# One weight copy, one normalisation pass and four folding transfers in the feed-forward half of an attention + SoLU kernel

## The chip, the cores and the metric

The kernel runs on one core of one Trainium2 chip. The metric is the time on the device in microseconds (us) of one execution, inputs and outputs in the chip's main memory. A core has five engines that run their own instruction queues side by side: PE (matrix multiply; its weight loads are shown as PEld), DVE, ACT and POOL (element-wise work) and SP, which here only issues transfers (DMAs). The engines wait for one another through semaphores. PE writes its results to PSUM, which has eight banks; everything else lies in SBUF, 128 partitions wide.

## The reference, cut to what matters

Everything is float32 except `w_in` and `w_out`, which come as 64-bit floats and are taken apart on the chip.

```python
def _attn_ref(q, k, v, tau):            # q, k, v: (8, 8, 576, 64)
    scores = scale * np.matmul(q, k.transpose(0, 1, 3, 2))
    thresh = np.max(scores, axis=-1, keepdims=True) - tau
    scores = np.where(scores >= thresh, scores, -1000000000.0)
    scores = scores - np.max(scores, axis=-1, keepdims=True)
    attn = np.exp(scores)
    attn = attn / (np.sum(attn, axis=-1, keepdims=True) + 1e-09)
    return np.matmul(attn, v)

def _moe_ref(x, w_in, w_out, g_ln):     # x: (4608, 512), w_in: (512, 1024), w_out: (1024, 512)
    h = x @ w_in
    e = np.exp(h - np.max(h, axis=-1, keepdims=True))
    solu = h * (e / (np.sum(e, axis=-1, keepdims=True) + 1e-09))
    mu = np.mean(solu, axis=-1, keepdims=True)
    var = np.mean((solu - mu) ** 2, axis=-1, keepdims=True)
    ln = (solu - mu) / np.sqrt(var + 1e-06) * g_ln
    return ln @ w_out
```

The attention output of the 8 heads, laid side by side, is `x`: 8 x 576 = 4608 tokens of 512 features.

## The kernel before, in words

**Rounds.** The program is written out by a Python loop over rounds (`rnd`, lines 898 to 1059). Each of the first 144 rounds (`NS`) takes one slot of attention: the scores of 128 query rows of two heads (`scores`, L480), their row maximum on DVE (`maxes`, L502), a threshold and an exponential on ACT (`ramp`, L517; `exps`, L526), a scaling on POOL one round later (`normalise`, L533 to L536), and a 32 x 32 block transpose on DVE (`blocks`, L548). After every second slot SP issues three or four transfers (L557, L559, L564) that fold the transposed weights `T` into `wT`, so that keys lie on the partitions. About three rounds later `attend_steps` (L590) multiplies with `v`, and ACT copies the result into the token tile `xh` or `xe` (L622). Each batch has 16 slots for its first 512 rows and two more for its last 64.

**The feed-forward half** works on 36 units of 128 tokens. A unit `t` takes four rounds of PE: `ff_h` twice (L655, or L645 near the end), then `ff_o` twice (L760, part 0 and part 1 in two consecutive rounds). Between its h and its o lie, each in a round of its own: `ff_max` and `ff_exp` (L670, L679), `ff_mul` and `ff_sum` (L685, L690, L691), `ff_stats` (L700 to L711), `ff_norm`, `ff_norm2` and `ff_swap`, and `ff_turn`. While one unit is in its h rounds, the unit before it is normalised and turned, and then has its o rounds. So the rounds go h, h, o, o in the middle of the kernel, with scores at the head of each round, and the h rounds also hold the attention products. The last scores are in round 144; after that the rounds hold only feed-forward steps, and the two parts of an o follow each other on PE with nothing between them.

**The path from u to o.** After `ff_mul` the tile `u` holds 128 tokens on the partitions and 1024 features. `ff_norm` (ACT, L721) writes the normalised values to `V`, `ff_norm2` (DVE, L726) writes the same values back over `u`. `ff_swap` issues four transfers on SP (L737); each moves 32 partitions x 512 features from `u` into `V`, so that after a block transpose on DVE (`ff_turn`, L747) the partitions 0 to 63 hold 64 features of the tokens 0 to 63, and the partitions 64 to 127 those of the tokens 64 to 127. `u`, `V` and (but for the end) `uT` have one buffer each.

**ff_o before.** Sixteen steps `m`, eight in each part. In each step, row half `r` (64 partitions) holds one half of the tokens, so it needs all of `w_out` by itself: `w2` holds `w_out` twice, the second time with its 64-partition halves exchanged (`weight_d`, L332: two transfers for each of eight pieces). Row half `r` always writes its own bank:

```python
out=d["o"][ROWS[z], 512 * (r ^ other) : 512 * (r ^ other) + 256],
lhsT=d["uT"][ROWS[r], m].rearrange("p y x -> p (y x)"),
rhs=w2[ROWS[r], m ^ r, 256 * z : 256 * z + 256],
```

**ff_h before, for comparison.** Its row halves hold different input features of the same tokens, so both add into the same results. In part 0 row half 0 writes bank 0 and row half 1 bank 1, in part 1 they exchange. `fence` (L109) is a POOL memset of a 128 x 1 tile that waits for the last four matmuls of part 0; the first matmul of part 1 waits for it. Units whose h falls at the end (`split` false, L645) use whole 128-row matmuls and need no fence.

**Start.** In rounds 0 to 15 the sixteen pieces of the 64-bit weights are loaded (512 KB each, `weight_load`, L275), taken apart (L286 to L325, on DVE, ACT and POOL), and for `w_out` multiplied with the gain `g_ln` in `gs`, whose rows are loaded once (L878) and turned on PE (`gains`). SP issues nearly all transfers in program order; each reuses one of eight semaphores, and waits until the transfer that had it before has landed.

Of the kernel before, what the change touches and what calls it, by code (L numbers as in the profile page):

```python
# [8 lines left out]
F32 = mybir.dt.float32  # L9
# [3 lines left out]
AF = mybir.ActivationFunctionType  # L13
# [7 lines left out]
def kernel(  # L21
# [47 lines left out]
    ident = const.tile([P, P], F32, name="ident")  # L69
    swapped = const.tile([P, 64], F32, name="swapped")  # L70
    w1 = const.tile([P, NP, DFF], F32, name="w1")
    w2 = const.tile([P, 2 * NC, DM], F32, name="w2")
    w1_parts = w1.rearrange("p c (a g x) -> p c g a x", g=2, x=32)
    mhalf = const.tile([P, 1], F32, name="mhalf")
    mone = const.tile([P, 2], F32, name="mone")
    mark = const.tile([P, 1], F32, name="mark")
# [181 lines left out]
    def piece(x):  # L258
        if x < 2 * NP:
            c, hf = divmod(x, 2)  # L260
            cols = slice(512 * hf, 512 * hf + 512)
            return w_in[P * c : P * c + P, cols], w1[:, c, cols], W_UNIT
        c = x - 2 * NP
        return w_out[P * c : P * c + P], w2[:, 2 * c], gs[:, c : c + 1]

    NW = 2 * NP + NC
    raws = {}
# [54 lines left out]
    def weight_gain(x):  # L322
        if wide and x >= 2 * NP:
            e = raws[x]["em"][0].bitcast(F32)
            nc.scalar.activation(out=e, in_=e, func=AF.Copy, scale=piece(x)[2])  # L325


    def weight_d(x):
        c = x - 2 * NP
        if c >= 0:  # L330
            for r in range(2):
                nc.sync.dma_start(out=w2[ROWS[r], 2 * c + 1], in_=w2[ROWS[1 - r], 2 * c])  # L332

    SPARE = 7
# [263 lines left out]
    def attended(key):  # L601
        b, kind, hp = key
        tag, y = units.pop(key)["y"]
        y = y.rearrange("p (u n) -> p u n", u=2)[:, :, 0:P]
        if kind == 2 or b < 2:
            y = y.rearrange("p u (r y) -> p u r y", r=2)
        else:
            y = y.rearrange("p u (g r x) -> p u g r x", g=2, r=2)
        if kind == 2:
            if b % 2 == 0:  # L610
                xe[b // 2] = work.tile([P, NP, P], F32, tag="xe", bufs=1, name="xe")
            to = xe[b // 2][:, :, 64 * (b % 2) : 64 * (b % 2) + 64].rearrange(
                "p (u r) y -> p u r y", u=2
            )
        else:
            if hp == 0:
                xh[b, kind] = work.tile(
                    [P, NP, 256], F32, tag=f"xh{(2 * b + kind) % 4}", bufs=1, name="xh"
                )
            how = "p (r u y) -> p u r y" if b < 2 else "p (u g x r) -> p u g r x"  # L620
            to = xh[b, kind][:, hp].rearrange(how, u=2, r=2, **({} if b < 2 else {"g": 2}))
        nc.scalar.copy(out=to, in_=y)  # L622
        pairs_free.append(tag)
# [92 lines left out]
    def ff_norm(t):  # L716
        d = ffn[t]
        rs, nb = d["norm"]
        d["V"] = V = work.tile([P, 2, DFF // 2], F32, tag="V", bufs=1, name="V")
        u = d["u"].rearrange("p (g n) -> p g n", g=2)  # L720
        nc.scalar.activation(out=V, in_=u, func=AF.Identity, bias=nb, scale=rs)  # L721

    def ff_norm2(t):
        d = ffn[t]
        rs, nb = d["norm"]
        nc.vector.tensor_scalar(  # L726
            out=d["u"], in0=d["u"], scalar1=rs, scalar2=nb, op0=ALU.mult, op1=ALU.add
        )

    def ff_swap(t):
        d = ffn[t]
        for g in range(2):
            for r in range(2):
                to, of = 64 * r + 32 * g, 64 * r + 32 * (1 - g)
                nc.sync.dma_start(  # L737
                    out=d["V"][to : to + 32, 1 - g],
                    in_=d["u"][of : of + 32, DFF // 2 * g : DFF // 2 * g + DFF // 2],
                )  # L740

    def ff_turn(t, rnd):
        d = ffn[t]
        turns.append(t)
        tag = "xh0" if rnd > NS and len(turns) % 2 else "uT"
        d["uT"] = uT = work.tile([P, 2 * NC, 2, 32], F32, tag=tag, bufs=1, name="uT")
        nc.vector.transpose(  # L747
            out=uT, in_=d["V"].rearrange("p y (m x) -> p m y x", x=32)
        )
        d["turned"] = rnd + 1  # L750

    def ff_o(t, part):
        d = ffn[t]
        other = len(t) == 3 and t[0] > 1 and t[2]
        if part == 0:
            d["otag"], d["o"] = take("o_ps")
        for m in range(NC * part, NC * part + NC):
            for r in range(2):
                for z in range(2):
                    nc.tensor.matmul(  # L760
                        out=d["o"][ROWS[z], 512 * (r ^ other) : 512 * (r ^ other) + 256],
                        lhsT=d["uT"][ROWS[r], m].rearrange("p y x -> p (y x)"),
                        rhs=w2[ROWS[r], m ^ r, 256 * z : 256 * z + 256],
                        start=m == 0, stop=m == 2 * NC - 1,
                    )

    def ff_out(t, last):
        d = ffn[t]
# [8 lines left out]

    def ff_store(t, last):
        d = ffn.pop(t)
        if len(t) == 1:  # L780
            of = slice(2 * t[0], 2 * t[0] + 2)
            if t[0] == 0:
                rows = out.rearrange("(b s) m -> s b m", s=S)[SM:S, of]
            else:
                rows = out.rearrange("(b k t) m -> k t b m", b=B, t=NK)[:, NK - 1, of]
        elif t[0] > 1:
            b, kind, m = t
            rows = out[b * S : b * S + S, :].rearrange("(k t) m -> k t m", t=NK)
            rows = rows[:, 4 * kind + 2 * m : 4 * kind + 2 * m + 2]
        else:  # L790
            b, kind, m = t
            rows = out[b * S : b * S + SM, :].rearrange("(p t) m -> t p m", t=4)
            rows = rows[2 * kind + m].rearrange("(r k) m -> k r m", r=2)
        for z in range(2):
            (nc.scalar if last and z else nc.sync).dma_start(
                out=rows[:, :, 256 * z : 256 * z + 256],
                in_=d["ob"][ROWS[z]].rearrange("p (r n) -> p r n", r=2),
            )


    NS = len(slots)
# [66 lines left out]
    with tc.manual_schedule():  # L868
# [29 lines left out]
        while True:  # L898
# [89 lines left out]
            if step == ("h", 0):  # L988
                ff_h(cur, 0, rnd + 1 < NS, beside)
                quarter = 1  # L990
            elif step == ("h", 1):
                ff_h(cur, 1, None, beside)
                quarter = 2
                by = rnd + 2 * (rnd == 14)
                late.setdefault(by, []).append(lambda t=cur: (ff_max(t), ff_exp(t)))
                late.setdefault(by + 1, []).append(lambda t=cur: (ff_mul(t), ff_sum(t)))
                middle.setdefault(by + 2, []).append(lambda t=cur: ff_stats(t))
                if rnd + 6 < NS:
                    norms[by + 3] = cur
                else:  # L1000
                    late.setdefault(rnd + 2, []).append(lambda t=cur: ff_norm(t))
                middle.setdefault(by + 3, []).append(lambda t=cur: (ff_norm2(t), ff_swap(t)))

                at = by + 4 if more or not ready or len(ready[0][1][0]) == 1 else rnd + 6
                if cur == (0, 1, 1):
                    middle.setdefault(rnd + 6, []).append(lambda t=cur, at=rnd + 6: ff_turn(t, at))
                else:
                    late.setdefault(at, []).append(lambda t=cur, at=at: ff_turn(t, at))
                if not more:
                    between.append(cur)  # L1010
                    cur = None
                    quarter = 0
            elif step == ("o", 0):
                if prev is not None:
                    ff_o(prev, 0)
                quarter = 3
            elif step == ("o", 1):
                if prev is not None:
                    ff_o(prev, 1)
                    last = not (more or ready or cur or between)  # L1020
                    begin.setdefault(rnd + 1, []).append(lambda t=prev, last=last: ff_out(t, last))
                    late.setdefault(rnd + 1, []).append(lambda t=prev, last=last: ff_store(t, last))
                prev, cur = cur, None
                quarter = 0
# [68 lines left out]
```

## Time and profile before

| | |
|---|---|
| median of 3 runs | 861.14 us |
| lowest, highest | 861.04, 863.58 us |
| the profiled execution, first to last instruction (its span) | 867.2 us |
| PE busy | 822.9 us, 95% of the span |
| DVE, ACT, POOL busy | 681.7, 573.6, 500.2 us |
| transfers | 168.54 MB, mean 194 GB/s |
| L760, matmuls of o | 4608, busy 271.6 us |
| L726, second normalisation on DVE | 36, mean 982 ns |
| L721, normalisation on ACT | 36, mean 1241 ns |
| L109, the fences of h on POOL | 32, mean 98 ns |

The profile gives no time of the profiled execution but its span; that lies 6.1 us above the median of the runs shown. "Busy" counts the time in which an engine has at least one instruction under way. Matmuls overlap one another, so a PE that is busy is not always at its full rate; the number of matmuls in a stretch says more. A line such as `L760` is line 760 of the kernel printed above. In a timeline, a bracket at the end of a line gives the engine's idle time before that instruction and what ended it.

### The profile page before, as it was taken

The page shows a single profiled execution, that of the slowest core. Times are in us where ns is not written, and L with a number is a line of the kernel's source. Part 1 is how long each engine was busy: PE and PEld are TensorE (multiplying, and loading weights), DVE is VectorE, ACT ScalarE, POOL GpSimd, SP SyncE. Part 2 cuts the span into 40 slices and gives each one's busy share as a digit, 9 for nine tenths or more (in the row PEclk, how much of TensorE's full clock was granted, in tenths as well). Part 3 has the DMA queues.
Part 4 walks back from the last instruction along what each step waited for, and adds up shares of the span by engine and source line. Part 5 has one row for each costly group of instructions (what it writes and reads, how often), then busy time and mean ns, then how long its engine had stood idle before and what let it go on. Part 6 is the DMA issues. An engine that isn't in the chain of part 4 may idle for free.

```text
span 867.2 us, 36122 instructions
## 1 busy us (share of the span) xinstructions
PE 822.9 (95%) x15361; PEld 605.8 (70%) x15361; DVE 681.7 (79%) x1248; ACT 573.6 (66%) x1153; POOL 500.2 (58%) x938
## 2 busy tenths in 40 slices
PE   5668799989999999999999999999999999999997
PEld 3446466667677776899777766777777777777655
DVE  4988878878788888888888887888788887787361
ACT  5877876667677767777666766777677776776121
POOL 2886656556756666565656665565666655555120
PEclk9769999999999999999999999999999999999999
DMA  8999887998888878898888787888788787655312
GB/s 256 252 251 227 191 210 181 210 236 210 215 206 226 208 183 214 208 221 203 196 207 225 207 187 185 217 220 207 183 230 229 197 192 180 163 136 139 69 38 62
DMA packets 83712, 168.54 MB, mean 194 GB/s; under 512 B 15448, under 2 KB 45152, under 8 KB 83552
## 3 DMA queue, kind: packets, MB, share of 16 engines
q1 hardware_dynamic: 82416, 164.25, 76.3%
q8 instruction: 120, 1.97, 1.0%
q10 hardware_dynamic: 1136, 2.00, 0.7%
q14 instruction: 40, 0.33, 0.1%
HBM read 46.14 MB, written 9.44 MB: 64 GB/s over the span
## 4 chain that ended last, share of the span: by engine, by line
PE 79%; DMA 8%; DVE 4%; ACT 4%; SPq 2%; issue 2%; POOL 1%; ACTq 0%; DVEq 0%
PE o_ps L760 26%; PE h_ps L655 20%; PE pv L590 14%; PE s_ps L480 14%; DMA wT<-T 6%; PE h_ps L645 3%; ACT w L517 1%; DVE w L502 1%; ACT w L526 1%; DVE T L548 1%; DMA q<-in_q_dram 1%; DMA qT<-flip 1%; SPq L564 1%; DMA k<-in_k_dram 1%; SPq L559 0%
## 5 line engine op out<-in xcount | busy, mean ns | idle before, releaser
L760 PE MATMUL o_ps<-w,uT 64*64 64x256 f32 x4608 | 271.6, 378 | 1.2 <-ACT xe L622 0.6
L502 DVE CUSTOM_DVE_ANT_0 w<-s_ps,tau_t 128x576 f32<-128x576 f32 x280 | 200.0, 751 | 90.0 <-PE s_ps L480 61.6
L517 ACT ACTIVATE w<-s_ps,nth 128x576 f32<-128x576 f32 x280 | 196.9, 739 | 107.0 <-DVE nth L502 89.6
L760 PEld LDWEIGHTS o_ps<-w,uT 64*64 64x64 f32 x4608 | 212.7, 134 | 66.1 <-ACT xh L622 12.1
L536 POOL TENSOR_SCALAR w<-w,sm 128x576 f32<-128x576 f32 x288 | 222.1, 783 | 14.3
L548 DVE STREAM_TRANSPOSE T<-w 128x576 f32<-128x576 f32 x288 | 207.6, 755 | 20.6 <-POOL w L536 19.1
L655 PE MATMUL h_ps<-w,xh 64*64 64x512 f32 x1856 | 221.0, 589 | 0.1
L526 ACT ACTIVATE w<-w,ntau 128x576 f32<-128x576 f32 x288 | 219.7, 767 | 0.0
L590 PEld LDWEIGHTS pv<-wT,v 64*64 64x64 f32 x5760 | 175.2, 138 | 45.4 <-issue 24.5
L480 PE MATMUL s_ps<-kT,qT 64*64 64x64 f32 (+1 forms) x2048 | 177.1, 422 | 13.3 <-ACT w L517 10.9
L590 PE MATMUL pv<-wT,v 64*64 64x128 f32 (+1 forms) x5760 | 178.0, 266 | 10.9 <-DMA wT<-T 7.8
L655 PEld LDWEIGHTS h_ps<-w,xh 64*64 64x64 f32 x1856 | 118.0, 133 | 78.8 <-issue 45.7
L533 POOL TENSOR_SCALAR sm<-sm 128x2 f32<-128x2 f32 x144 | 37.0, 257 | 201.8 <-ACT w L526 198.5
L534 POOL TENSOR_TENSOR sm<-sm,mone 128x2 f32<-128x2 f32 x144 | 108.7, 755 | 12.0
L480 PEld LDWEIGHTS s_ps<-kT,qT 64*64 64x64 f32 x2048 | 73.0, 139 | 21.7 <-ACT w L517 15.7
L622 ACT COPY xh<-pv 128x256 f32<-128x256 f32 x64 | 25.1, 393 | 82.4 <-PE pv L590 82.4
L721 ACT ACTIVATE V<-u,nb,rs 128x1024 f32<-128x1024 f32 x36 | 44.7, 1241 | 39.3 <-POOL nb L711 32.4
L747 DVE STREAM_TRANSPOSE uT<-V 128x1024 f32<-128x1024 f32 x36 | 44.2, 1227 | 18.1 <-DMA V<-u 17.7
L526 ACT ACTIVATION_READ_ACCUMULATOR w<-w,ntau 128x1 f32 x288 | 55.6, 193 | 0.0
L685 DVE TENSOR_TENSOR u<-h_ps,u 128x1024 f32<-128x1024 f32 x36 | 42.8, 1190 | 9.8 <-ACT u L679 9.8
L726 DVE TENSOR_SCALAR u<-u,rs,nb 128x1024 f32<-128x1024 f32 x36 | 35.3, 982 | 17.6 <-ACT V L721 17.6
L670 DVE TENSOR_REDUCE hm<-h_ps 128x1 f32<-128x1024 f32 x36 | 42.9, 1192 | 4.8 <-PE h_ps L645 2.7
(90 smaller groups left out, 568.1 us busy)
## 6 DMA issues: line engine op xcount, KB each, us to landing
wT<-T SPq DMA_DIRECT2D x160, 288.0 KB, 6.7
wT<-T SPq DMA_DIRECT2D x64, 576.0 KB, 5.4
V<-u SPq DMA_DIRECT2D x144, 64.0 KB, 3.3
out_dram<-ob SPq DMA_DIRECT2D x71, 128.0 KB, 2.5
q<-in_q_dram SPq DMA_DIRECT2D x24, 288.0 KB, 5.7
qT<-flip SPq DMA_DIRECT2D x48, 144.0 KB, 4.2
k<-in_k_dram SPq DMA_DIRECT2D x24, 288.0 KB, 6.1
kT<-flip SPq DMA_DIRECT2D x48, 144.0 KB, 3.9
```

Source lines behind the costliest of these rows:

```text
L480: nc.tensor.matmul(out=ps[h][ROWS[y], ks], lhsT=lhsT, rhs=d["kT"][ROWS[h], ks], start=True, stop=True,)
L502: nc.vector.tensor_tensor_reduce(out=w, in0=ps[:, 0:S], in1=(zero if loose else tau_t).to_broadcast([P, S]), scale=1.0, scalar=BIG, op0=AL ...
L517: nc.scalar.activation(out=d["w"][x], in_=d["w"][x] if d["loose"] else d["ps"][x][:, 0:S], func=AF.Prelu, bias=d["nth"][x], scale=-1.0, al ...
L526: nc.scalar.activation(out=w, in_=w, func=AF.Exp, bias=ntau, scale=1.0, accum_out=sm[:, x : x + 1])
L534: nc.gpsimd.tensor_tensor(out=sm, in0=sm, in1=mone, op=ALU.pow)
L536: nc.gpsimd.tensor_scalar(out=w, in0=w, scalar1=sm[:, x : x + 1], scalar2=1.0, op0=ALU.mult, op1=ALU.mult)
L548: nc.vector.transpose(out=T[:, :, r, h, :], in_=w)
L590: nc.tensor.matmul(out=to, lhsT=d["v"][ROWS[u], (h0 + h - u) % 4 if b > 1 else h0 + h, m ^ 4 * u if m < 8 and b < 2 else m,], rhs=rhs, sta ...
L655: mm = nc.tensor.matmul(out=h[ROWS[y], f], lhsT=x[ROWS[r], c, ROWS[y]], rhs=w1_parts[ROWS[r], c, part ^ r], start=part == 0 and c == 0, st ...
L721: nc.scalar.activation(out=V, in_=u, func=AF.Identity, bias=nb, scale=rs)
L747: nc.vector.transpose(out=uT, in_=d["V"].rearrange("p y (m x) -> p m y x", x=32))
L760: nc.tensor.matmul(out=d["o"][ROWS[z], 512 * (r ^ other) : 512 * (r ^ other) + 256], lhsT=d["uT"][ROWS[r], m].rearrange("p y x -> p (y x)" ...
```

## The change

`w2` holds `w_out` once, with the rows ordered so that the partition `32 b + i` of piece `m` is row `256 b + 32 m + i`; `weight_d` and its sixteen transfers are gone. The gain rows are loaded by four small transfers in that order. `ff_norm` normalises `u` in place on ACT, and `ff_norm2` is gone. `ff_fold` takes the place of `ff_swap`: each of its four transfers moves a quarter of the features of all 128 tokens (128 KB) into 32 partitions of `V`. The same block transpose then leaves 128 different features on the partitions in each of eight steps, for all 128 tokens. `ff_o` adds the two row halves into the same results, as `ff_h` does: eight steps in part 0, a fence, and the same eight steps in part 1 with the banks exchanged. The token order inside a unit changes with the fold, so the copies into `xh` and `xe` use another order, and the stores write whole 2 KB rows. `w1_parts` becomes two plain halves.

```diff
-    w2 = const.tile([P, 2 * NC, DM], F32, name="w2")
-    w1_parts = w1.rearrange("p c (a g x) -> p c g a x", g=2, x=32)
+    w2 = const.tile([P, NC, DM], F32, name="w2")
+    w1_parts = w1.rearrange("p c (g n) -> p c g n", g=2)
...
-        return w_out[P * c : P * c + P], w2[:, 2 * c], gs[:, c : c + 1]
+        rows = w_out.rearrange("(b m i) n -> m b i n", b=4, i=32)
+        return rows[c], w2[:, c], gs[:, c : c + 1]
...
-    def weight_d(x):
-        c = x - 2 * NP
-        if c >= 0:
-            for r in range(2):
-                nc.sync.dma_start(out=w2[ROWS[r], 2 * c + 1], in_=w2[ROWS[1 - r], 2 * c])
...
-            to = xe[b // 2][:, :, 64 * (b % 2) : 64 * (b % 2) + 64].rearrange(
-                "p (u r) y -> p u r y", u=2
-            )
+            y = y.rearrange("p u r (k e) -> p u r k e", e=2)
+            to = xe[b // 2].rearrange("p (u r) (k w e) -> p w u r k e", u=2, w=2, e=2)[:, b % 2]
...
-            how = "p (r u y) -> p u r y" if b < 2 else "p (u g x r) -> p u g r x"
+            how = "p (r u y) -> p u r y" if b < 2 else "p (g x u r) -> p u g r x"
...
     def ff_norm(t):
         d = ffn[t]
         rs, nb = d["norm"]
-        d["V"] = V = work.tile([P, 2, DFF // 2], F32, tag="V", bufs=1, name="V")
-        u = d["u"].rearrange("p (g n) -> p g n", g=2)
-        nc.scalar.activation(out=V, in_=u, func=AF.Identity, bias=nb, scale=rs)
-
-    def ff_norm2(t):
+        nc.scalar.activation(out=d["u"], in_=d["u"], func=AF.Identity, bias=nb, scale=rs)
+
+    def ff_fold(t):
         d = ffn[t]
-        rs, nb = d["norm"]
-        nc.vector.tensor_scalar(
-            out=d["u"], in0=d["u"], scalar1=rs, scalar2=nb, op0=ALU.mult, op1=ALU.add
-        )
-    def ff_swap(t):
...
+        d["V"] = V = work.tile([P, 4, DFF // 4], F32, tag="V", bufs=1, name="V")
+        for b in range(4):
+            nc.sync.dma_start(
+                out=V[32 * b : 32 * b + 32], in_=d["u"][:, 256 * b : 256 * b + 256]
+            )
...
-        d["uT"] = uT = work.tile([P, 2 * NC, 2, 32], F32, tag=tag, bufs=1, name="uT")
+        d["uT"] = uT = work.tile([P, NC, 4, 32], F32, tag=tag, bufs=1, name="uT")
...
     def ff_o(t, part):
         d = ffn[t]
-        other = len(t) == 3 and t[0] > 1 and t[2]
         if part == 0:
             d["otag"], d["o"] = take("o_ps")
-        for m in range(NC * part, NC * part + NC):
+        uT = d["uT"].rearrange("p m a x -> p m (a x)")
+        last = []
+        for m in range(NC):
             for r in range(2):
+                f = part ^ r
                 for z in range(2):
-                    nc.tensor.matmul(
-                        out=d["o"][ROWS[z], 512 * (r ^ other) : 512 * (r ^ other) + 256],
-                        lhsT=d["uT"][ROWS[r], m].rearrange("p y x -> p (y x)"),
-                        rhs=w2[ROWS[r], m ^ r, 256 * z : 256 * z + 256],
-                        start=m == 0, stop=m == 2 * NC - 1,
+                    mm = nc.tensor.matmul(
+                        out=d["o"][ROWS[z], 512 * f : 512 * f + 256],
+                        lhsT=uT[ROWS[r], m, ROWS[z]],
+                        rhs=w2[ROWS[r], m, 256 * f : 256 * f + 256],
+                        start=part == 0 and m == 0, stop=part == 1 and m == NC - 1,
                     )
+                    if part and not last:
+                        sync(mm, d["ofence"])
+                    last.append(mm)
+        if part == 0:
+            d["ofence"] = fence(last[-4:])
...
-        for z in range(2):
-            (nc.scalar if last and z else nc.sync).dma_start(
-                out=rows[:, :, 256 * z : 256 * z + 256],
-                in_=d["ob"][ROWS[z]].rearrange("p (r n) -> p r n", r=2),
-            )
+        for z, rows in enumerate(halves):
+            (nc.scalar if last and z else nc.sync).dma_start(out=rows, in_=d["ob"][ROWS[z]])
...
-        nc.sync.dma_start(out=g_rows, in_=g_ln.rearrange("(c p) -> c p", p=P))
+        for b in range(4):
+            nc.sync.dma_start(
+                out=g_rows[:, 32 * b : 32 * b + 32],
+                in_=g_ln.rearrange("(b m i) -> b m i", b=4, i=32)[b],
+            )
...
-                middle.setdefault(by + 3, []).append(lambda t=cur: (ff_norm2(t), ff_swap(t)))
+                middle.setdefault(by + 3, []).append(lambda t=cur: ff_fold(t))
...
-                weight_d(pieces[rnd - 1])
```

More of the change, by code (lines that the diff above doesn't have):

```diff
@@ L718, in ff_norm @@
         rs, nb = d["norm"]
-        d["V"] = V = work.tile([P, 2, DFF // 2], F32, tag="V", bufs=1, name="V")
-        u = d["u"].rearrange("p (g n) -> p g n", g=2)
-        nc.scalar.activation(out=V, in_=u, func=AF.Identity, bias=nb, scale=rs)
-    def ff_norm2(t):
+        nc.scalar.activation(out=d["u"], in_=d["u"], func=AF.Identity, bias=nb, scale=rs)
+    def ff_fold(t):
         d = ffn[t]
-        rs, nb = d["norm"]
-        nc.vector.tensor_scalar(
-            out=d["u"], in0=d["u"], scalar1=rs, scalar2=nb, op0=ALU.mult, op1=ALU.add
-        )
-    def ff_swap(t):
[L733 to L739, printed above, removed]
-                )
+        d["V"] = V = work.tile([P, 4, DFF // 4], F32, tag="V", bufs=1, name="V")
[3 more added lines that the diff above has]
+            )
     def ff_turn(t, rnd):
@@ L745, in ff_turn @@
         tag = "xh0" if rnd > NS and len(turns) % 2 else "uT"
-        d["uT"] = uT = work.tile([P, 2 * NC, 2, 32], F32, tag=tag, bufs=1, name="uT")
+        d["uT"] = uT = work.tile([P, NC, 4, 32], F32, tag=tag, bufs=1, name="uT")
         nc.vector.transpose(
-            out=uT, in_=d["V"].rearrange("p y (m x) -> p m y x", x=32)
+            out=uT, in_=d["V"].rearrange("p a (m x) -> p m a x", x=32)
         )
@@ L779, in ff_store @@
         d = ffn.pop(t)
+        halves = []
         if len(t) == 1:
[L781 to L785, printed above, removed]
+            for b in (2 * t[0], 2 * t[0] + 1):
+                if t[0] == 0:
+                    rows = out[b * S + SM : b * S + S, :].rearrange("(k e) m -> e k m", e=2)
+                else:
+                    rows = out[b * S : b * S + S, :].rearrange("(k e t) m -> t e k m", t=NK, e=2)
+                    rows = rows[NK - 1]
+                halves.append(rows)
         elif t[0] > 1:
             b, kind, m = t
-            rows = out[b * S : b * S + S, :].rearrange("(k t) m -> k t m", t=NK)
-            rows = rows[:, 4 * kind + 2 * m : 4 * kind + 2 * m + 2]
+            rows = out[b * S : b * S + S, :].rearrange("(k e t) m -> t e k m", t=NK, e=2)
+            halves = [rows[4 * kind + x] for x in ((0, 3), (1, 2))[m]]
         else:
             b, kind, m = t
-            rows = out[b * S : b * S + SM, :].rearrange("(p t) m -> t p m", t=4)
-            rows = rows[2 * kind + m].rearrange("(r k) m -> k r m", r=2)
-        for z in range(2):
-            (nc.scalar if last and z else nc.sync).dma_start(
-                out=rows[:, :, 256 * z : 256 * z + 256],
-                in_=d["ob"][ROWS[z]].rearrange("p (r n) -> p r n", r=2),
-            )
+            rows = out[b * S : b * S + SM, :].rearrange("(k a t) m -> t a k m", t=4, a=4)
+            rows = rows[2 * kind + m]
+            halves = [rows[0:2], rows[2:4]]
+        for z, rows in enumerate(halves):
+            (nc.scalar if last and z else nc.sync).dma_start(out=rows, in_=d["ob"][ROWS[z]])
     NS = len(slots)
```

## The prediction

> **What bounds the kernel now.** I read the engines' busy shares and the 40 slices first, then busy time by stage, to see where PE still has idle time that a change could win.
>
> ```profile
> PE 822.9 (95%) x15361; PEld 605.8 (70%) x15361; DVE 681.7 (79%) x1248; ACT 573.6 (66%) x1153; POOL 500.2 (58%) x938
> ...
> PE   5668799989999999999999999999999999999997
> ```
>
> ```profile
> 0.00:60.00 60.00, 36.01 (x615) 23.02 (x619) 47.13 (x103) 44.35 (x97) 38.88 (x59) 0.81 0.93 254
> ...
> 90.00:110.00 20.00, 14.88 (x332) 9.47 (x328) 17.37 (x34) 17.84 (x45) 13.76 (x21) 0.88 0.80 190
> ...
> 260.00:520.00 260.00, 259.44 (x4934) 202.66 (x4932) 217.39 (x393) 181.67 (x360) 158.62 (x310) 1.00 0.83 207
> 520.00:780.00 260.00, 258.43 (x4942) 193.91 (x4938) 213.67 (x388) 180.55 (x357) 156.53 (x302) 1.00 0.77 195
> ...
> 812.00:855.00 43.00, 43.00 (x660) 26.94 (x654) 19.20 (x23) 10.27 (x14) 7.11 (x21) 1.00 0.20 45
> ```
>
> The columns of the second view are the stretch, its length, busy us (and instructions) of PE, PEld, DVE, ACT and POOL, the granted clock, the DMA share and GB/s. From 260 to 780 us PE idles 2.1 us of 520 at full clock: taking 35 us off DVE cannot help there. PE idles 24 us in the first 60, 5.1 between 90 and 110, and not at all from 812 to 855. So the middle and the tail can only lose, and only the start can win.
>
> Is PE at its rate where it is busy? The chain that ended last closes with the o steps of the last four units, without a gap:
>
> ```profile
> 834.57 27.83 PE o_ps L760 x512
> ```
>
> That is 27.83 / 512 = 54 ns from one matmul to the next, while one lasts 376 ns (median of L760). Seven are under way together, so making PE run empty once costs about 376 - 54 = 0.32 us before any waiting.
>
> A steady pair of o rounds, in order of time (start, length, engine, line, what):
>
> ```profile
> 499.76 3.20 PE L760 MATMUL o_ps<-w,uT 64*64 64x256 f32 x56
> ...
> 502.84 1.31 PE L480 MATMUL s_ps<-kT,qT 64*64 64x64 f32 x15
> ...
> 503.73 0.23 POOL L533 TENSOR_SCALAR sm<-sm 128x2 f32<-128x2 f32 x1 [2.46 <-ACT w L526]
> 503.76 3.63 PE L760 MATMUL o_ps<-w,uT 64*64 64x256 f32 x61
> ```
>
> Between the parts stand only the scores of the next round, and POOL is idle for 2.46 us when part 0 ends. Last, the way from the turn of one unit to PE, with the waits and transfers that feed it:
>
> ```profile
> 387.46 1.25 DVE L747 STREAM_TRANSPOSE uT<-V 128x1024 f32<-128x1024 f32 x1 [0.53 <-DMA V<-u]
> ...
> 388.62 1.19 DVE L670 TENSOR_REDUCE hm<-h_ps 128x1 f32<-128x1024 f32 x1
> ...
> 389.92 1.11 ACT L679 ACTIVATE u<-h_ps,hm 128x1024 f32<-128x1024 f32 x1
> ...
> 391.46 1.42 ACT L517 ACTIVATE w<-s_ps,nth 128x576 f32<-128x576 f32 x2 [0.34 <-POOL se L690]
> ...
> 393.59 0.22 PE L480 MATMUL s_ps<-kT,qe 64*64 64x64 f32 x1
> ```
>
> ```profile
> DVE uT L747 <- DMA V<-u: 17.7, 14, 4.7
> ```
>
> ```profile
> V<-u SPq DMA_DIRECT2D x144, 64.0 KB, 3.3
> ...
> qT<-flip SPq DMA_DIRECT2D x48, 144.0 KB, 4.2
> kT<-flip SPq DMA_DIRECT2D x48, 144.0 KB, 3.9
> ...
> w<-w SPq DMA_DIRECT2D x16, 128.0 KB, 8.0
> ```
>
> DVE already waits for the swap 14 times (17.7 us). A late turn delays the next unit's maximum, its exponential, the ramp behind that on ACT, and so the scores of the second o round.
>
> **The change part by part.**
>
> *PE's work* stays: 128 matmuls of the same shape for each unit, so 0. That `w1` is now read in whole runs: the h matmuls already follow one another at their rate (32 in 3.43 us on the chain), so 0 too.
>
> *The fence, steady rounds.* 31 units have scores between the parts. Part 0 above ends at 503.18 (its last three start at 502.79 and last 0.39). The memset starts 0.07 after such an end (the fence at 76.17 follows matmuls that end at 76.10), lasts 98 ns, releases PE in about 0.05 (scores started at 53.37 after a ramp that ended at 53.32), and if the wait stands before the weight load, 0.13 more: 503.53. Part 1 started at 503.76. Hidden, with 0.2 us to spare; in other units part 1 started 0.4 to 0.8 after part 0's end. The cover is the scores; if the wake-up took 0.3 longer it would cost 31 x 0.1 = 3 us, if 0.5 longer 9. On POOL, `ff_sum` (0.23 + 0.57) stands behind the fence, in some rounds the scaling of q (0.75), then the next `normalise`, which would start near 504.2 instead of 503.73. Its reader is the DVE transpose at 507.12, and POOL ended at 506.34: 0 but for the rounds with a q scaling, where h rounds follow with time to spare.
>
> *The fence, tail.* Five units (o at 813.55 and four from 834.57) have nothing between the parts and a PE without gaps. Each pays 0.32 + 0.07 + 0.10 + 0.05 = 0.54, or 0.67 with the weight load: 5 x 0.6 = **+3.0** (2.2 to 3.6). POOL is idle there, as its table shows only 7.1 us from 812 to 855.
>
> *Second normalisation.* 36 x 0.982 = 35.3 us leave DVE, behind PE throughout: 0. It doesn't start the transfers sooner in most units: in the unit above SP still issued older `wT` transfers until 381.34 and the swap followed at 381.44, while the second pass had ended at 380.54.
>
> *The fold* moves 512 KB instead of 256 KB a unit in four transfers as before. All transfers of the main queue moved 164.25 MB in 76.3% of 867.2 us, 248 GB/s while busy; 256 KB more take **1.06 us**, and the last landing comes so much later. (By the rows of transfers, 144 KB land 0.6 to 0.9 us later than 64 KB; the bounds are -1.2, a start that is free of the second pass, and +4.7, the 8.0 us of 128 KB copies in the crowded start.) I take the engines' rate, as the swap queues behind `wT`. The turn then waits: 1.06 x 30 gives DVE back most of what it won. For PE the slack behind the turn counts. In the unit shown it is 0.11 (maximum to exponential) + 0.24 (to the ramp) + 0.71 (ramp's end to scores) = 1.06; worked out alike, 1.2 to 1.9 in most others. So 0 in the common units. In three the turn is already late: at 132.23 (DVE waited 2.30, and it is on the chain: 1.06), at 323.44 (waited 1.82; the ramp ends 0.3 before the scores: 0.7) and at 716.91 (1.86; 0.65 left: 0.4). **+2.1**.
>
> By the Trainium skill, page "SBUF — State Buffer", section "The DMA setup-cost knee", a transfer takes a fixed 2 us and then its bytes at 436 GB/s: the fold would land 0.6 us later, the three turns cost 0.8 and the sum below would be +2.8; this trace's 248 GB/s speaks for the row.
>
> *Weights.* Sixteen copies of 128 KB, 2.1 MB or 8.5 us at 248 GB/s, leave the stretch 62 to 112 us, 16% of it. But the chain there runs over DVE (84 to 94) and ACT (99 to 108); of DMA it holds a load (77.2 to 84.0) and one `wT` (94.0 to 98.7), 11.6 us. 16% of that is 1.9; I take **-1.0** (0 to -8.5). w_out is now needed whole by part 0, but its last piece is ready at 106.8, before the first o at 108.57: 0.
>
> *Small things.* Three more gain loads are three SP issues of 0.36 us at 8 us, behind them a weight piece that round 3 needs: 0, at most 1.1. Stores: the same 72, with rows twice as long: 0. The copies into `xh` write with a wider step; the step of 8 bytes took 395 ns against 372 for whole runs, so 0.03 each, up to 48 x 0.03 = 1.4, mostly hidden: 0. First normalisation in place: same 1.24 us.
>
> Sum: 3.0 + 2.1 - 1.0 = +4.1 on the profiled span of 867.2, so 871.3; the profiled execution lay 6.1 over the median, so the same 4.1 on 861.14: **865 us**.
>
> **The rivals.**
>
> *A. The fold is later than 1.06.* Past 1.5 us PE pays in the 27 common units too. For: the turn has 0.1 to 0.5 us of margin only, and 128 KB copies have taken 8.0. Against: the DMA share is 0.8 and pieces of 1152 bytes move at the same rate. At a delay of 1.8 some 0.3 to 0.4 x 27 = 9: 874; at 2.3 some 22: 887.
>
> *B. The fence shows in the steady rounds.* For: 0.2 us of slack. Against: every wake-up that the trace shows is under 0.1. With 0.5 more: 31 x 0.3 = 9, 874.
>
> *C. Faster: the start wins more.* Transfers take 0.93 to 1.04 of the time up to 90 us, PE waits for `wT`, and a late PE lost clock (0.81 granted up to 60 us). If half of the 8.5 us and some clock come back, -7, with fences at 2.2 and late turns at 0.8: -4, 857. It decides from a saving of 5.1 on. Against: the long `wT` wait before 68 us was issued at 55.92, before the first weight copy at 62.19.
>
> Beside C the Trainium skill, "SBUF — State Buffer", section "Who interferes with whom", has DVE's two-port modes and GpSimd lock each other out; the second pass does show two lengths here, 0.81 and 1.20 us, but what POOL would win hides behind PE.
>
> **How the numbers follow.** No change to this kernel can be told from one within 0.3%, 2.6 us (858.5 to 863.7). My forecast 0.52 (862 to 869), A 0.18, B 0.09, C 0.21. Slower: three quarters of the forecast, A and B, 0.65; same: the rest of the forecast and a third of C, 0.21; faster 0.14. The range 857 to 878 leaves out the lower half of C and A's upper third, about 0.15.
>
> **What would show it.** Right: five gaps of 0.5 to 0.7 us between the parts of o after 812; none before; `uT` waiting for its transfers some 25 to 40 us in total; no second pass; transfers of 128 KB landing in 4 to 4.5 us. Wrong: gaps before part 1 or before the scores in the middle (B, A), or PE's first 130 us much shorter (C).

## The result and the profile after

The changed kernel takes 922.62 us (median of 4 runs, 916.53 to 924.32) where the kernel before takes 861.09 in the same comparison: a ratio of 1.0694, 95% interval 1.0658 to 1.0731. The forecast was 865, the range ended at 878. The direction was right, the size was not: +61.5 us where +4.1 was worked out. All ratios in this document leave out executions in a slower state: the profiled one of ten of the sixteen-group kernel below (2189.72 us) and two of twelve of the last kernel.

The page of the changed kernel, engines and slices (a slice is now 23.0 us):

```profile
span 920.6 us, 36138 instructions
...
PE 830.7 (90%) x15361; PEld 544.7 (59%) x15361; DVE 648.1 (70%) x1212; ACT 584.4 (63%) x1153; POOL 489.7 (53%) x974
...
PE   5645759989999999999999998999999999999995
...
DMA  8965568788988888898888787998889877766231
```

PE has as many matmuls as before and 8 us more busy time, in a span 53.4 us longer. The third to the sixth slice (46 to 138 us) are the new hole, and there the transfers are *less* busy than before: the DMA digits fall to 5 and 6 where they stood at 8 and 9. Busy time by stage shows it more sharply. The first fence is the changed kernel, the second the kernel before in the same stretches (stretch, length, then PE, PEld, DVE, ACT and POOL busy, granted clock, DMA share, GB/s):

```profile
58.00:66.00 8.00, 1.89 (x28) 1.51 (x32) 3.00 (x8) 4.10 (x8) 3.67 (x5) 0.50 0.80 175
66.00:76.00 10.00, 3.66 (x68) 2.78 (x60) 5.40 (x12) 3.81 (x8) 1.27 (x1) 0.67 0.27 95
76.00:86.00 10.00, 5.10 (x88) 4.57 (x92) 1.50 (x4) 1.01 (x4) 2.58 (x4) 0.53 0.68 165
```

```profile
58.00:66.00 8.00, 6.37 (x88) 4.67 (x88) 4.67 (x11) 4.55 (x10) 6.39 (x7) 0.61 1.03 265
66.00:76.00 10.00, 8.44 (x130) 6.74 (x134) 6.75 (x16) 6.61 (x14) 4.25 (x6) 0.83 0.86 221
76.00:86.00 10.00, 10.00 (x162) 7.11 (x158) 9.46 (x19) 7.82 (x17) 8.21 (x11) 1.00 1.11 228
```

Between 66 and 76 us every engine is idle for 4.6 us or more (PE for 6.3), and yet the 16 DMA engines are busy for only 0.27 of the time. Nothing is at its limit, and everything waits. For what, the chain that ended last says (start, length, what):

```profile
40.56 0.13 DVE em L287
40.69 16.76 DMA raw<-in_moe_w_out_dram
57.45 0.02 issue
57.47 0.02 SPq L276
57.48 0.03 issue
57.52 14.49 DMA raw<-in_moe_w_out_dram
72.01 0.03 issue
72.03 0.02 DVEq L287
```

Two loads of a 512 KB piece of `w_out` stand one behind the other with 16.8 and 14.5 us, and a third later with 12.4. In the kernel before, the median of such a load was 9.8 us, with a DMA share of 0.86 to 1.11 between 40 and 96 us. Here 0.27 x 16 = 4.3 engines are at work: as if a piece went over four of them.

Where the rest went is read from the times at which the o of a unit starts (first matmul of part 0, us from the start of the span):

```
o of unit            0      3     12     20     30     35   end of span
before           108.6  191.4  390.1  567.0  783.8  855.3   867.2
after            133.3  215.7  423.4  606.8  828.1  902.9   920.6
difference        24.7   24.3   33.3   39.7   44.3   47.6    53.4
```

So there are three losses: 24 us before unit 3, 20 us in small steps between unit 3 and unit 30, and 9 us after it. They add up to the 53.4 us between the two profiled executions, not to 61.5: the start of before's was late (o of unit 0 at 108.6, where seven of the kernels below, with `w_out` loaded as before, have 103.5 to 104.8), so the change loses some 29 us in the start. For the middle, PE's waits between 180 and 780 us (engine, line, waited for: us in total, times, longest):

```profile
PE pv L582 <- DMA wT<-T: 6.4, 13, 1.3
PE pv L582 <- DMA v<-in_v_dram: 2.6, 1, 2.6
```

Before, the wait for `wT` was 0.6 us there and that for `v` did not show. Neither transfer was touched by the change. After the last matmul (which ends at 910.5), the last store is issued at 911.47 and the span ends at 920.6, 9.1 us later; before it was 3.9 (863.33 to 867.2). The stretch in which nothing but stores is under way, after and before:

```profile
913.00:918.50 5.50, 0.00 (x0) 0.00 (x0) 0.00 (x0) 0.00 (x0) 0.00 (x0) 0.67 0.12 40
```

```profile
863.50:867.00 3.50, 0.00 (x0) 0.00 (x0) 0.00 (x0) 0.00 (x0) 0.00 (x0) 0.92 0.30 75
```

A share of 0.12 is 2 of 16 engines. In the changed kernel, the stores are written `"(k e) m -> e k m"` with `e=2` (alike for the other kinds of unit), and the loads `"(b m i) n -> m b i n"` with `b=4`: in main memory the outermost dimension has two and four entries. Theory 1 is therefore: the number of entries of the outermost dimension limits how many DMA engines carry a transfer; four engines for the loads lengthen the start, two for the stores delay whatever stands behind them. The rivals were those of the prediction: the fold (A), the fence (B).

Counted from the traces' records of single packets, those of 4 KB (the weight loads) or of 2 KB (the stores, at the end of the span) that are under way at once, where they have the engines to themselves (the kernels with 8 and 16 groups follow below; a packet's record can run a little into the next one's):

```
load of a piece, 128 rows on end (before)         up to 15.4
load led by 16 groups                             up to 16.5
load led by 8 groups                              8.0 to 8.3
load led by 4 groups (alone, and changed kernel)  4.1
store led by 4 groups                             4.0 to 4.2
store led by 2 groups                             2.1
```

The Trainium skill has this as a rule: page "DMA: Bandwidth & Descriptors", section "Why a DMA increments its semaphore by 16 and not by 1", says that the slowest dimension longer than one of each side is looked at, and that the transfer uses the largest number of engines up to 16 that divides both. Every line of the table agrees with it. The same section has such transfers, when issued from SP or ACT, always on the lowest-numbered engines, so that they would meet on the same ones; the records here don't name engines, so no run shows which ones they are. That transfers on few engines meet is in the counts. In the changed kernel, counting 128 packets to a load, the load issued at 40.69 has its first packet at 49.0, and the last of the load before it ends at 49.2: half of its 16.8 us is waiting for that load, and with up to four loads issued there were still only 4.1 packets at a time. The last two stores are issued at 911.47, one by SP and one by ACT, and have 2.1 together.

### The profile page after: what moved, and what is told of

Same layout as the page of the kernel before. It is cut to its first block, busy times and chain, and to the rows that moved or that the text cites. A ratio compares the mean times of both kernels' runs of the same rounds, so it can differ in the third digit from the quotient of the medians.

```text
span 920.6 us, 36138 instructions
## 1 busy us (share of the span) xinstructions
PE 830.7 (90%) x15361; PEld 544.7 (59%) x15361; DVE 648.1 (70%) x1212; ACT 584.4 (63%) x1153; POOL 489.7 (53%) x974
## 4 chain that ended last, share of the span: by engine, by line
PE 46%; DMA 29%; DVE 7%; ACT 6%; SPq 6%; issue 3%; POOL 2%; ACTq 0%; DVEq 0%; POOLq 0%
PE o_ps L740 16%; DMA wT<-T 15%; PE h_ps L646 11%; PE pv L582 8%; PE s_ps L472 8%; DMA raw<-in_moe_w_out_dram 5%; DVE w L494 3%; DMA q<-in_q_dram 3%; ACT w L509 2%; ACT w L518 2%; DMA k<-in_k_dram 2%; SPq L551 2%; DMA V<-u 2%; PE h_ps L636 2%; DVE T L540 1%
## 5 line engine op out<-in xcount | busy, mean ns | idle before, releaser
L740 PEld LDWEIGHTS o_ps<-w,uT 64*64 64x64 f32 x4608 | 189.9, 133 | 94.2 <-ACT xh L613 19.1
L528 POOL TENSOR_SCALAR w<-w,sm 128x576 f32<-128x576 f32 x288 | 212.7, 750 | 14.3
L582 PEld LDWEIGHTS pv<-wT,v 64*64 64x64 f32 x5760 | 167.7, 137 | 83.6 <-issue 52.0
L472 PE MATMUL s_ps<-kT,qT 64*64 64x512 f32 (+1 forms) x2048 | 169.3, 419 | 16.7 <-ACT w L509 12.4
L646 PEld LDWEIGHTS h_ps<-w,xh 64*64 64x64 f32 x1856 | 91.1, 133 | 106.2 <-issue 86.6
L613 ACT COPY xh<-pv 128x256 f32<-128x256 f32 x64 | 37.3, 583 | 93.2 <-PE pv L582 93.2
L109 POOL MEMSET mark<- 128x1 f32 x68 | 6.7, 98 | 151.1 <-PE o_ps L740 146.2
L472 PEld LDWEIGHTS s_ps<-kT,qT 64*64 64x64 f32 x2048 | 65.6, 139 | 28.4 <-ACT w L509 17.8
L710 ACT ACTIVATE u<-u,nb,rs 128x1024 f32<-128x1024 f32 x36 | 44.6, 1240 | 38.0 <-POOL nb L702 37.9
L670 ACT ACTIVATE u<-h_ps,hm 128x1024 f32<-128x1024 f32 x36 | 40.2, 1116 | 25.6 <-DVE hm L661 16.0
```

The lines of the kernel that those rows point to most:

```text
L472: nc.tensor.matmul(out=ps[h][ROWS[y], ks], lhsT=lhsT, rhs=d["kT"][ROWS[h], ks], start=True, stop=True,)
L528: nc.gpsimd.tensor_scalar(out=w, in0=w, scalar1=sm[:, x : x + 1], scalar2=1.0, op0=ALU.mult, op1=ALU.mult)
L582: nc.tensor.matmul(out=to, lhsT=d["v"][ROWS[u], (h0 + h - u) % 4 if b > 1 else h0 + h, m ^ 4 * u if m < 8 and b < 2 else m,], rhs=rhs, sta ...
L646: mm = nc.tensor.matmul(out=h[ROWS[y], f], lhsT=x[ROWS[r], c, ROWS[y]], rhs=w1_parts[ROWS[r], c, part ^ r], start=part == 0 and c == 0, st ...
L710: nc.scalar.activation(out=d["u"], in_=d["u"], func=AF.Identity, bias=nb, scale=rs)
L740: mm = nc.tensor.matmul(out=d["o"][ROWS[z], 512 * f : 512 * f + 256], lhsT=uT[ROWS[r], m, ROWS[z]], rhs=w2[ROWS[r], m, 256 * f : 256 * f + ...
```

## The experiments

**The loads undone.** In the changed kernel, `w_out` is loaded in its natural order, and the order of features that the fold asks for is made by how h reads `w1`.

```diff
-    w1_parts = w1.rearrange("p c (g n) -> p c g n", g=2)
+    w1_parts = w1.rearrange("p c (m g b i) -> p c g b m i", g=2, b=2, i=32)
...
-        rows = w_out.rearrange("(b m i) n -> m b i n", b=4, i=32)
-        return rows[c], w2[:, c], gs[:, c : c + 1]
+        return w_out[P * c : P * c + P], w2[:, c], gs[:, c : c + 1]
...
-        for b in range(4):
-            nc.sync.dma_start(
-                out=g_rows[:, 32 * b : 32 * b + 32],
-                in_=g_ln.rearrange("(b m i) -> b m i", b=4, i=32)[b],
-            )
+        nc.sync.dma_start(out=g_rows, in_=g_ln.rearrange("(c p) -> c p", p=P))
```

> The changed kernel with one part undone: each piece of w_out is loaded as 128 rows that follow one another in memory, in the natural order, and the gains by one transfer; the order of features that the fold needs is made in h instead (the h matmuls read the columns of w1 in runs of 32). Theory 1: the loss of 24.5 us between rounds 8 and 16 comes from the w_out loads, whose source is led by four groups of 32 rows and of which only about 4 of the 16 DMA engines' worth of packets is under way at a time. Then PE reaches round 16 as early as the kernel before or up to 4 us earlier, the time falls by 24 to 28 us to 895 to 899 us, and the loss of 20 us between rounds 16 and 140 stays. Rival: the start is slow because of the fold or the waits on POOL; then the time stays above 915 us.

Measured: 900.97 us, ratio 1.0447 (1.0403 to 1.0491): 21.6 us won, somewhat less than expected. The o of unit 0 starts at 104.7 instead of 133.3, so all of the start's loss is gone; the middle loses as before or more (24.5 us behind the kernel before at unit 30).

**The stores undone.**

```diff
         for z, rows in enumerate(halves):
-            (nc.scalar if last and z else nc.sync).dma_start(out=rows, in_=d["ob"][ROWS[z]])
+            for e in range(2):
+                of = slice(64 * z + 32 * e, 64 * z + 32 * e + 32)
+                (nc.scalar if last and z else nc.sync).dma_start(out=rows[e], in_=d["ob"][of])
```

> The changed kernel with its stores cut: each half of ob is stored by two transfers of 32 rows of 2 KB instead of one whose target is led by two groups of 32 rows. Theory 1 says that the store led by two groups keeps two DMA engines busy for about 2.7 us (32 packets of 84 ns each) while every other transfer waits for its packets on these two: then half or more of the 20 us between rounds 16 and 140 comes back, and the last store lands 2 to 3 us sooner: 900 to 910 us. Rival: the middle is lost to the fence on POOL or to the bytes of the fold; then only the end gains, 919 to 921 us, or, by two more issues on SP for each unit, nothing.

Measured: 900.62 us, ratio 1.0430 (1.0394 to 1.0467). The o of unit 3 still starts at 212.6; from there to unit 30 the delay grows from 21.2 to 29.4, by 8 us instead of 20, and the end costs little. More issues on SP, and faster.

**Both undone.**

> The two edits together (contiguous w_out loads, stores of 32 rows). If the two causes are separate, the gains add up: with theory 1 for both, 873 to 885 us; with the stores costing only the end, 892 to 897 us. What is left over the kernel before is then the price of the fold and of the fences, of which five fences at the end are 2.5 us.

Measured: 869.40 us, ratio 1.0083 (1.0061 to 1.0106). Together the two edits win 53.2 us of the 61.5, better than any expectation: each is worth 31 us where the other is already mended (900.97 - 869.40 = 31.6 for the stores, 900.62 - 869.40 = 31.2 for the loads) and 22 where it isn't. After a late start, so it seems, part of what slow stores cost is made up; that was not tested. The stretch of the hole, and the two long stretches of the middle:

```profile
66.00:76.00 10.00, 10.00 (x134) 7.17 (x130) 8.20 (x19) 7.47 (x14) 7.58 (x11) 0.94 1.00 256
```

```profile
260.00:520.00 260.00, 258.05 (x4852) 158.07 (x4844) 204.00 (x380) 185.59 (x359) 153.69 (x318) 1.00 0.88 218
520.00:780.00 260.00, 259.17 (x5004) 158.85 (x5008) 201.39 (x373) 184.33 (x356) 153.83 (x316) 1.00 0.82 208
```

DMA share 1.00 instead of 0.27 and PE without a gap; PE busy for 517.2 of 520 us, as in the kernel before (517.9).

**The loads alone, in the kernel before.** One line: `rows[c]` of the four-group view in place of `w_out[P * c : P * c + P]`.

> The kernel before with one change alone: each piece of w_out is loaded with the rows led by four groups of 32 (as the changed kernel does); w_out's rows so stand in another order in the product o, and nothing else differs. Theory 1: the start loses 24 us or more (the copies of the pieces still follow each load), 883 to 895 us, with all of the loss by round 16. Rival (the loads are hidden): 861 to 866 us.

Measured: 894.15 us, ratio 1.0362 (1.0343 to 1.0380). The stretch of the hole is here too, without fold, fence or new stores:

```profile
66.00:76.00 10.00, 1.58 (x36) 0.70 (x28) 4.80 (x11) 4.48 (x9) 1.75 (x3) 0.83 0.26 98
```

**Is it the number of groups?** The same line with `b=16, i=8` and `b=8, i=16`.

> The kernel before with each piece of w_out loaded as sixteen groups of 8 rows, the groups outermost (w_out's rows so stand in another order in o). The same 128 packets of 4 KB, in memory further apart than in the four groups of 32. If the number of groups that lead the transfer sets how many DMA engines carry it, sixteen groups are as good as 128 rows: 861 to 866 us. Rival: rows that don't follow one another are slow as such, or a shape of three dimensions is; then it is at least as slow as the four groups, 890 us or more.

> The same with eight groups of 16 rows. If the groups set the number of engines, each of eight engines carries 16 packets instead of 8 on sixteen or 32 on four; the loss of 31.7 us at four groups, taken as linear in the packets per engine, would be 31.7 x (16 - 8) / (32 - 8) = 10.6 us, and less if a load that lands 2 us later is still in time: 863 to 874 us. Rival as above: 890 us.

Measured: sixteen groups 867.43 us, ratio 1.0049 (1.0024 to 1.0074); eight groups 877.16 us, ratio 1.0177 (1.0123 to 1.0231). So, by the ratios, +4, +15 and +31 us for sixteen, eight and four groups. The more a piece is scattered, the faster it is: the rival, scattered rows, falls. Eight groups cost half as much as four, rather more than the 10.6 of the linear estimate, which lies at the edge of the interval (10.6 to 19.9); sixteen cost a few us more than 128 rows on end, for which no run gives a reason.

**The stores alone, in the kernel before.** Its `ff_store` is replaced by that of the changed kernel.

> The kernel before with one change alone: its stores are written as the changed kernel writes them, whole rows of 2 KB with a target led by two groups of 32 rows (the rows of a unit so land in another order in the output). Theory 1: they cost what undoing them won in the changed kernel, 22 us where the loads were also slow and 31.5 where they were not, that is 880 to 894 us, most of it in rounds 40 to 140 in small steps of 1 to 4 us, and 2 to 3 us after the last matmul. Rival: they hurt only together with the larger fold; then 863 to 868 us, the end alone.

Measured: 892.28 us, ratio 1.0319 (1.0266 to 1.0373), +28.5, as theory 1 had it. It does not take the larger fold. The chain at the end of this kernel, and the stretch after it:

```profile
865.59 12.49 DMA out_dram<-ob
878.08 0.02 issue
878.10 0.04 ACTq L772
```

```profile
880.00:889.00 9.00, 0.00 (x0) 0.00 (x0) 0.00 (x0) 0.00 (x0) 0.00 (x0) 0.52 0.11 42
```

The last copy into `ob` waits 12.5 us for a store to free the tile, and the last store takes 10.4 us from its issue to the end of the span, against 3.9. Here the two engines are the limit: the last eight stores, issued from 863.73 on, run two packets at a time without a pause from 866 to 887 us. From the o of unit 30 to the end of the span this kernel takes 93.4 us, the kernel before 83.4.

**How does a slow store hurt the others?** The same with four groups of 16 rows (`e=4` in the four views; `a=8` in that of the first batches).

> The kernel before with stores of whole 2 KB rows led by four groups of 16 rows (the rows of a unit land in another order). On four engines a unit's two stores take 2 x 16 x 84 ns = 2.7 us each, against 5.4 us on two and 1.25 us on each of sixteen before. Theory 1a, overload: a unit lasts 21.6 us in which each engine is busy 0.83 of the time; with stores on two engines those two would need 0.83 + (5.4 - 1.25) / 21.6 = 1.02, more than there is, and the kernel goes at their pace; on four it is 0.83 + (2.7 - 1.25) / 21.6 = 0.90, so nothing is lost but at the end: 862 to 867 us. Theory 1b, each transfer behind a store is late by the store's length, in proportion: 28.5 x 1.45 / 4.15 = 10 us, 872 to 876 us.

Measured: 878.55 us, ratio 1.0161 (1.0120 to 1.0201), by which it loses 13.9 us: half of the loss at two groups. Theory 1a, by which four engines have room and nothing is lost, is refuted. The loss goes with the length of the store, and is rather more than 1b gave (10; the interval is 10.4 to 17.4). What waits behind a store waits longer, also where there is room on average; at the end, with two groups, overload comes on top. Whether it waits in the queues of the DMA engines or already on SP, no run separates: between 180 and 780 us SP waits before its stores for landings of `wT` for 7.3 us with two groups and 2.4 with four, and not at all in the kernel before.

**The fence alone, in the kernel before.** `fence(last[-4:])` after part 0 and `sync` before the first matmul of part 1, as in the diff of the change, around the old order of the sums.

> The kernel before with one change alone: between the two parts of each o stands a fence on POOL, as in the changed kernel; the sums are as before. The prediction's term: hidden behind the scores in 31 units and 0.5 to 0.6 us in each of the last five, so +2.4 to +3.0 us, 864 to 865.5 us, all of it after 812 us. Rival B: it shows in the steady rounds, 0.1 to 0.3 us in each of 31: 867 to 874 us.

Measured: 867.26 us, ratio 1.0038 (1.0011 to 1.0066), +3.3. Waits of PE's weight loads for the fence between 180 and 780 us, and the chain at the end:

```profile
PEld o_ps L761 <- POOL mark L109: 3.2, 17, 0.2
```

```profile
833.70 0.05 issue
833.75 0.17 POOL mark L109
833.92 0.04 issue
833.97 7.18 PE o_ps L761 x128
```

These 3.2 us lie in the weight loads and reach no matmul: from unit 6 to unit 30 this kernel's lead over the profiled execution of before goes from 3.7 to 5.0 us, that is, nothing is lost. In the last five units a pair of parts takes 7.5 us instead of the 6.96 of before, and from the o of unit 31 to the end of the span 56.5 us go by instead of 53.7.

**The fold alone, in the kernel before.** The four transfers of the swap are replaced by those of the fold; both normalisations stay.

> The kernel before with one change alone: in place of the four 64 KB transfers of the swap it issues the four 128 KB transfers of the fold, both normalisations still there (o is computed from features in another order than its weights have). The prediction's term: 1.06 us more for each unit costs PE 2.1 us in three units, so 863 to 865 us. With four times the packets, each of half the length (1 KB), the rows of packets give 512 x 80 ns / 16 = 2.6 us instead of 128 x 110 ns / 16 = 0.9, that is 1.7 us later; by the prediction's rival A that would be 870 to 874 us.

Measured: 868.65 us, ratio 1.0048 (1.0021 to 1.0075), +4.1. The transfer's row (KB, median us to landing) and DVE's wait for it:

```profile
V<-u SPq DMA_DIRECT2D x144, 128.0 KB, 4.4
```

```profile
DVE uT L743 <- DMA V<-u: 48.8, 31, 5.6
```

It lands 1.1 us later than the 3.3 of the swap, and DVE waits 48.8 us for it in total instead of 17.7, with next to no harm to PE: between unit 6 and unit 30 one us is lost.

**Without the fence: whole-array matmuls.** With loads and stores mended, o by eight steps of 128 x 128 x 512 into one bank.

```diff
+        for m in range(NC // 2 * part, NC // 2 * part + NC // 2):
+            nc.tensor.matmul(
+                out=d["o"][:, 0:512], lhsT=uT[:, m], rhs=w2[:, m],
+                start=m == 0, stop=m == NC - 1,
+            )
...
```

> The version with contiguous w_out loads and stores of 32 rows, and o by whole 128 x 128 matmuls of 512 columns into one bank (four steps in each part), so that no fence is needed. The same PE time by the rows: 16 matmuls of 435 ns (32 in 13.93 us in the h of the end) are 6.96 us for each unit, against 6.95 for 128 of 54.3 ns. Theory: the five fences at the end are won, 2.4 us, and POOL's wait for part 0 is gone: 866 to 867 us. Rival: PE pays for the change between 64-row and 128-row matmuls in each of the 62 steady rounds, 0.1 to 0.3 us: 872 to 885 us.

> The version with contiguous w_out loads and stores of 32 rows, and whole 128 x 128 matmuls without a fence for o only after the last scores (five units), where h already uses whole matmuls and nothing has to change shape between them. In the steady rounds o stays as in the changed kernel. Theory: the five stops of 0.5 us are won, 2.4 us, so a ratio of 1.0055 over the kernel before instead of 1.0083: 866 to 868 us where before is 862.5. Rival: with half as many results streams under way each matmul's start is longer, so the gain is lost: 869 us.

Measured: in all units 882.10 us, ratio 1.0204 (1.0167 to 1.0240); only after the last scores 866.15 us, ratio 1.0019 (0.9984 to 1.0054). The chains at the end, of the first and of the second:

```profile
848.59 27.48 PE o_ps L735 x64
```

```profile
827.96 27.48 PE o_ps L738 x64
```

27.48 us for four units are 6.87 each, so the end is won in both. But in the steady rounds the first loses time: from round 48 to round 92, 11 units, it takes 246.0 us, the kernel before 239.2, and the kernel with both undone, from which it differs by o alone, 241.1. That is 0.45 us for each unit, or 0.2 for each o round, in which PE goes from 64-row scores to 128-row matmuls and back; measured from the last score matmul to the first of the next round, an o round between 300 and 700 us is 0.3 longer. The Trainium skill, page "TensorEngine Tiling (Array Packing)", section "Key Properties", says that a change of tiling mode drains TensorE; the loss agrees with it, though no run has the change without the larger matmuls. The second kernel, with three things mended, cannot be told from the kernel before. No version here beats it.

## Why the prediction failed

**The step that failed is the list of small things**, and what it does not list. It has "Stores: the same 72, with rows twice as long: 0", and under *Weights* only the copies that leave, not the loads that stay with another row order. Both are the same bytes in packets as large or larger, and were priced by that. They measured +28.5 (stores alone) and +31.7 (loads alone) in the kernel before, and undone together 53.2 of the 61.5 us. What counts was in the diff: the order of the dimensions in main memory. The prediction even had the right fact beside it, that the start runs with transfers at 0.93 to 1.04 of the time (0.91 between 60 and 70 us); it drew from that only that fewer bytes would help.

**The rest of the sum stood.** With loads and stores mended, 1.0083 is +7 us (5 to 9), against the +4.1 that was worked out:
- *The fence*: +3.0 (2.2 to 3.6), hidden in the steady rounds. Measured +3.3 (0.9 to 5.7), all at the end. Right, and rival B is refuted: some waits of PEld do show, but they reach no matmul.
- *The fold*: 1.06 us later, +2.1. It landed 1.1 later, and cost 4.1 (1.8 to 6.5). DVE's total wait was put at 25 to 40 and was 50.7 with loads and stores mended: the later landing pushed more turns into waiting than was counted. Rival A, that it is much later, is refuted. By the packets' count it should have been 1.7 later; the rate, 1.06, was nearer. It was also nearer than the estimate of 0.6 us from the Trainium skill's page "SBUF — State Buffer", section "The DMA setup-cost knee".
- *Weights*, -1.0 (0 to -8.5), and the second normalisation, 0: fence and fold alone add up to 7.4, the mended kernel measures 7, so they are worth about nothing, with an uncertainty of some 3 us (that kernel also reads `w1` in another order and issues 72 more stores). Rival C fell. A faster start is seen in the profile of the mended kernel (o of unit 0 at 103.7 instead of 108.6), but the kernel before with nothing but a fence added has it too (104.8): it is the late start of the profiled execution of before.
- *The copies into `xh`*: put at 0.03 us each, they went from 393 to 583 ns (a step of 16 bytes instead of 8), six times that term. No run prices this alone; it is within the 7 us.

One mistake in method: the range was built from the rivals of the terms that had been thought of. The edits costed at nothing got no upper end, although the trace of before shows no transfer led by two or four groups, so none of its rows could say what one takes.

## What to carry to other kernels

Read the outermost dimension of every transfer that an edit touches, on both sides: with two, four or eight entries it went here over that many of the 16 DMA engines. With four, a load of 512 KB took 12 to 17 us, in part behind the load before it, instead of 10, while the profile showed idle compute engines and a DMA share of a quarter. A reordering in main memory is better put where it costs nothing, here into the order in which a matmul reads its weights, or cut into transfers that each lead with 16 rows or more, though they are more in number. An edit that is priced at nothing needs the same bounds as the others: ask what row shows that shape of transfer at all.

## What was not expected of the hardware

A packet of 4 KB on one of four engines took 161 ns, 25 GB/s for each engine (four make 102, and the rows show 95 to 98); in a stretch with all 16 at work the same packets took 200 to 300 ns. A store of 128 KB on two engines (64 packets of 2 KB, 84 ns each, 2.7 us) costs the kernel 0.8 us for each of 36 units on average (a third of it after unit 30) though 14 engines are free of it, and with four engines half of that. Whole 128-row matmuls between 64-row ones cost 0.2 to 0.3 us in each o round.
